# A chunked mLSTM with two feed-forward layers: the state's output matmuls move to the scores, the state update to the outputs, and a second chunk opens with six half-width blocks

## The chip, the core and the metric

The kernel runs on one core of one Trainium2 chip. The metric is the device time of one execution in microseconds (us), the median of the runs shown; less is better. Before the change it is 881.96 us over 3 runs (881.24 to 885.67). TensorE is written PE (its weight loads PEld), VectorE DVE, ScalarE ACT, GpSimd POOL, and SP is the queue that issues the DMAs.

## The reference

```python
for t in range(S):                        # B, H, S, D = 4, 8, 768, 40
    m_new = np.maximum(f_gate[:, :, t] + m, i_gate[:, :, t])
    f_stab = np.exp(f_gate[:, :, t] + m - m_new)
    i_stab = np.exp(i_gate[:, :, t] - m_new)
    C = f_stab * C + i_stab * np.einsum('bhd,bhe->bhde', vt, kt)
    n = f_stab * n + i_stab * kt
    h_tilde = np.einsum('bhde,bhe->bhd', C, qt)
    denom = np.maximum(np.abs(np.einsum('bhd,bhd->bh', n, qt)), 1.0)
    y[:, :, t] = sigmoid(o_gate[:, :, t]) * h_tilde / denom
x = y as (3072 tokens, 320)
x = (sigmoid(x @ w_gate) * (x @ w_val)) @ w_out            # d_ff 1536
h = x @ w_in
out = (h * clip(h + 3, 0, 6) / 6) @ w_out2                 # d_ff 2048
```

## The kernel before

The 768 tokens are cut into 6 chunks (0 to 5) of 128; with 4 batches that is 24 pieces of attention, each over 8 heads. Inside a chunk the recurrence is a masked product; between chunks a state of 40 x 41 words for each head (`cst`; the 41st column is the normaliser) is carried. All attention matmuls take fp32 operands; those of the feed-forward layers take fp32r words split into a high and a low part.

One piece of attention (chunk c, batch b) is three functions. They are called here by letters:

- **S** (`att0`, line 299): the scores, 8 matmuls of 40 x 128 by 128 columns, in two PSUM banks, one for even and one for odd heads (L303). DVE makes the decay matrix `dec` by two scans (L320, after a DMA that spreads a row over the partitions), scales v into `vi` and `vd`, and multiplies the scores into `dec` (L333).
- **I** (`att1`, line 340): for c > 0 the state's output part **O**, 16 matmuls with 32 output rows and 82 columns (L349): two heads' queries are stacked in 128 rows, and `cst` holds the two heads' states side by side with zero blocks. Then the chunk's own output, 32 matmuls of 41 columns (L360). DVE adds both into `y` (L373, L376), divides and gates it into `yo` (L380 to L387).
- **T** (`att2`, line 397): three transposes of `yo` (L402); then the state update **C**, 8 matmuls with 40 output rows (L409). ACT and DVE write the transposed piece as high and low part `xh`, `xl` (L419, L420), and DVE renews `cst` in two halves (L429, L432).

The first feed-forward layer goes over 12 hidden blocks for each chunk. One block of one chunk is a **step**: 16 matmuls for gate and value (`m1_h`, L443 to L450), ACT's sigmoid and DVE's product `g` (L470), a split into `gh` and `gl` (L456, L457), and one step later 8 matmuls into three accumulators (`m1_out`, L485, L495). In chunks 0 and 1 the first 4 blocks are done by halves (256 columns: batches 0 and 1, then batches 2 and 3), so that a chunk can begin before its last two batches are ready. `quota` says how many pieces of attention are emitted ahead of each step; from chunk 2 on it is one a step, and the pieces are a chunk ahead of the feed-forward layer. The order of pieces is (c,b) S, (c,b-1) T, (c,b) I.

During chunk 0 the weights are also converted: 64-bit words come in through SP, and ACT and DVE make fp32 and split it (L105 to L154). The second feed-forward layer (L601 on) begins when all chunks have gone through the first, with no attention beside it.

PSUM's 8 banks are three pools: 3 `mm` for `m1_h`, 3 `acc`, and 2 `att` for attention. The tiles `qk`, `vko` and `dec` of a piece have two buffers each; the loads for a piece are emitted behind T of the piece two before it and go out on SP in the order `qk`, `dec`, `vko`, each when its buffer is free. Each engine runs its instructions in the order in which a scheduler has written them when the kernel is built. These lines set the half-width blocks and the pieces:

```python
halves = 4
n = halves if c < 2 else 0
quota = [2, 2] + [1] * 4 + [0, 1] * 4 + [1] * (n_first - 14)
quota += [1] * (len(steps) - len(quota))
```

Of the kernel before, what the change touches and what calls it, by code (L numbers as in the profile page):

```python
# [8 lines left out]
F32 = mybir.dt.float32  # L9
# [10 lines left out]
L = 128  # L20
NC = S // L
# [11 lines left out]
def mlstm_then_two_gated_ffn(  # L33
# [33 lines left out]
    def any_ps():  # L67
        k = banks_used[0] % 8
        banks_used[0] += 1
        return ps_mm() if k < 3 else ps_acc() if k < 6 else ps_att()  # L70
# [7 lines left out]
    cst = const.tile([P, B, NP, 2 * D1], F32, name="cst")  # L78
# [191 lines left out]
    nc.gpsimd.memset(cst, 0.0)  # L270
# [26 lines left out]
    def att0(c, b, ps):  # L297
        a = at[c, b]
        qk, dec = a["qk"], a["dec"]
        s_ps = [ps(), ps()]  # L300
        for h in range(H):
            p0 = 64 * (h % 2)
            nc.tensor.matmul(  # L303
                out=s_ps[h % 2][:, (h // 2) * L : (h // 2 + 1) * L],
                lhsT=qk[p0 : p0 + D, 1, h // 2, :],
                rhs=qk[p0 : p0 + D, 0, h // 2, :],
                start=h < 2,
                stop=h >= H - 2,
                skip_group_check=True,
            )  # L310
        vko_t = a["vko"]
        vi = ap.tile([P, H, D1], F32, tag="vi", name="vi")
        v_h = vko_t[:, 0, :].rearrange("p (h d) -> p h d", d=D)
# [12 lines left out]
        a["vi"] = vi  # L326
        if c < NC - 1:
            vd = ap.tile([P, H, D1], F32, tag="vd", name="vd")
            scale_heads(vd, vi, dec[:, :, L - 1 : L], c == 0 and b > 0)
            a["vd"] = vd  # L330
        for n in range(2):
            x = dec.rearrange("p (n two) l -> p two n l", two=2)[:, n]
            nc.vector.tensor_tensor(  # L333
                out=x, in0=s_ps[n].rearrange("p (n l) -> p n l", l=L), in1=x, op=ALU.mult
            )

        with tc.issue_after(first_exp):
            nc.scalar.activation(out=vko_t[:, 2, :], in_=vko_t[:, 2, :], func=AF.Sigmoid)

    def att1(c, b, ps):  # L340
        a = at[c, b]
        dec, vi = a["dec"], a["vi"]

        halves = [slice(t, t + 32) for t in range(0, L, 32)]
        if c > 0:
            o_ps = ps()
            for n in range(NP):
                for tt in halves:
                    nc.tensor.matmul(  # L349
                        out=o_ps[tt, n * 2 * D1 : (n + 1) * 2 * D1],  # L350
                        lhsT=a["qk"][:, 0, n, tt],
                        rhs=cst[:, b, n, :],
                        start=n == 0,
                        stop=n == NP - 1,
                        skip_group_check=True,
                    )
        i_ps = ps()
        for h in range(H):
            for tt in halves:
                nc.tensor.matmul(  # L360
                    out=i_ps[tt, h * D1 : (h + 1) * D1],
                    lhsT=dec[:, h, tt],
                    rhs=vi[:, h, :],
                    start=h == 0,
                    stop=h == H - 1,
                    skip_group_check=True,
                )
        i_v = i_ps[:, : H * D1].rearrange("p (h d) -> p h d", d=D1)
        y = ap.tile([P, H, D1], F32, tag="y", name="y")
        den = ap.tile([P, H, 1], F32, tag="den", name="den")  # L370
        if c > 0:
            o_v = o_ps[:, : H * D1].rearrange("p (h d) -> p h d", d=D1)
            nc.vector.tensor_tensor(  # L373
                out=y, in0=o_v, in1=gT[:, c, b].to_broadcast([P, H, D1]), op=ALU.mult
            )
            nc.vector.tensor_tensor(out=y, in0=y, in1=i_v, op=ALU.add)  # L376
        else:
            nc.scalar.copy(out=y, in_=i_v)
# [6 lines left out]
        scale_heads(y[:, :, 0:D], y[:, :, 0:D], den, c == 1 or c == 0 and b < 2)  # L385
# [9 lines left out]
        a["yo"] = yo  # L395

    def att2(c, b, ps):
        a = at.pop((c, b))
        yo = a["yo"]
        x_ps = ps()  # L400
# [4 lines left out]
        if c < NC - 1:  # L405
            c_ps = ps()
            for h in range(H):
                p0 = 64 * (h % 2)
                nc.tensor.matmul(  # L409
                    out=c_ps[p0 : p0 + D, (h // 2) * D1 : (h // 2 + 1) * D1],  # L410
                    lhsT=a["vko"][:, 1, h * D : (h + 1) * D],
                    rhs=a["vd"][:, h, :],
                    start=h < 2,
                    stop=h >= H - 2,
                    skip_group_check=True,
                )
# [6 lines left out]
        if c < NC - 1:  # L423
            for j in range(2):
                pp = slice(64 * j, 64 * j + D)
                cv = cst[pp, b, :, j * D1 : (j + 1) * D1]
                c_v = c_ps[pp, : NP * D1].rearrange("p (n d) -> p n d", d=D1)
                if c > 0:
                    nc.vector.tensor_tensor(  # L429
                        out=cv, in0=cv, in1=gend[pp, c, b].to_broadcast([D, NP, D1]), op=ALU.mult  # L430
                    )
                    nc.vector.tensor_tensor(out=cv, in0=cv, in1=c_v, op=ALU.add)  # L432
                else:
                    nc.scalar.copy(out=cv, in_=c_v)
# [133 lines left out]
    halves = 4  # L568

    def tile_steps(c):  # L570
        n = halves if c < 2 else 0
        by_half = [(c, f, slice(j * T // 2, (j + 1) * T // 2)) for j in range(2) for f in range(n)]
        return by_half + [(c, f, slice(0, T)) for f in range(n, F1)]
# [11 lines left out]
    quota = [2, 2] + [1] * 4 + [0, 1] * 4 + [1] * (n_first - 14)  # L585
    quota += [1] * (len(steps) - len(quota))
    before = []
    for i, (c, f, ts) in enumerate(steps):
        if i == halves - 1:
            for b in range(2):  # L590
                att_load(1, b)
                dec_load(1, b)
        for _ in range(quota[i]):
            if pieces:
# [3 lines left out]
                (att0, att1, att2)[piece](cp, b, ps_att)  # L598
# [10 lines left out]
        if c == 0:  # L609
            work(1 if i < 2 * halves else 2, n_w1)  # L610
# [79 lines left out]
def _layout(q, k, v, i_gate, f_gate, o_gate, moe_w_gate, moe_w_val, moe_w_out, moe2_w_in, moe2_w_out):  # L690
# [21 lines left out]
    def words(w):  # L712
# [6 lines left out]
        "vko": np.stack([tokens(v), tokens(k), tokens(o_gate)], axis=3),  # L719
# [26 lines left out]
```

## Time and profile before

| | |
|---|---|
| median of 3 runs | 881.96 us |
| the profiled execution: its own time, its span | 883.74 us, 881.8 us |
| PE busy, weight loads busy | 844.9 us (96%), 721.9 us (82%) |
| DVE busy | 536.0 us (61%) |
| ACT busy | 362.2 us (41%) |
| mean share of the 16 DMA engines' bandwidth moved | 96 GB/s |

How to read it: the busy time of PE has the pipelined ends of matmuls in it, so that 96% does not mean that PE could do no more; the distance from one matmul's start to the next is what a matmul costs in a row. The span has four stretches: until 41.66 us the first pieces of attention alone; until 132.14 us chunk 0 of the first layer, with the conversion of weights; until 537.81 us its other chunks, which have attention beside them up to 461 us; and then the second layer.

### The profile page before, as it was taken

To read this page: it belongs to the slowest core of one execution; us is meant where nothing else is said; L and a number is where in the kernel's file an instruction comes from. 1 tells how busy PE (TensorE), PEld (TensorE's weight loads), DVE (VectorE), ACT (ScalarE), POOL (GpSimd) and SP (SyncE) were. 2 spreads that over 40 slices of the span, in tenths; PEclk is the share of its full clock that TensorE was granted. 3 is DMA by queue.
4 is the path that set the end of the run, shared out by engine and by line. 5 is a ranking of instruction groups with operands and counts; after the bars stand their busy time and mean duration, and the time that the engine had idled before them with its cause. 6 is when DMAs were issued, how large, how long until landed. Compare 5 with 4: busy or idle time off the path is not lost.

```text
span 881.8 us, 16306 instructions
## 1 busy us (share of the span) xinstructions
PE 844.9 (96%) x6805; PEld 721.9 (82%) x6805; DVE 536.0 (61%) x955; ACT 362.2 (41%) x728; POOL 2.5 (0%) x8
## 2 busy tenths in 40 slices
PE   2699998999999999999999999999999999999998
PEld 2587777887778778788888888999999999999997
DVE  7999997666777786777645554434343353443443
ACT  5874654222332233242325445334343343433433
POOL 1000000000000000000000000000000000000000
PEclk9999999999999999999999999999999999999999
DMA  9745453232443544435302231001010010000000
GB/s 324 269 143 183 149 184 130 83 108 71 150 143 135 183 159 153 161 132 196 135 1 71 90 105 72 1 1 66 1 56 11 1 66 1 30 1 1 30 1 30
DMA packets 25208, 84.43 MB, mean 96 GB/s; under 512 B 2608, under 2 KB 5872, under 8 KB 25136
## 3 DMA queue, kind: packets, MB, share of 16 engines
q1 hardware_dynamic: 25088, 83.31, 27.4%
q8 instruction: 53, 0.87, 0.4%
q14 instruction: 19, 0.16, 0.1%
q10 hardware_dynamic: 48, 0.10, 0.0%
HBM read 69.40 MB, written 13.99 MB: 95 GB/s over the span
## 4 chain that ended last, share of the span: by engine, by line
PE 82%; DVE 11%; DMA 3%; ACT 2%; issue 1%; SPq 0%; DVEq 0%; ACTq 0%
PE mm L447 11%; PE mm L449 11%; PE mm L448 11%; PE acc L485 9%; PE mm L443 6%; PE mm L450 5%; PE acc L652 5%; PE acc L651 5%; PE acc L650 5%; PE acc L495 3%; PE att L303 2%; DVE dec L320 2%; PE att L652 2%; PE att L651 2%; PE att L650 2%
## 5 line engine op out<-in xcount | busy, mean ns | idle before, releaser
L447 PE MATMUL mm<-xh,w 128*128 128x512 f32 (+1 forms) x512 | 194.4, 380 | 0.0
L449 PE MATMUL mm<-xh,w 128*128 128x512 f32 (+1 forms) x512 | 193.9, 379 | 0.0
L448 PE MATMUL mm<-xl,w 128*128 128x512 f32 (+1 forms) x512 | 193.8, 378 | 0.0
L456 ACT CAST gh<-g 128x512 fp32r<-128x512 f32 (+1 forms) x176 | 105.7, 600 | 177.3 <-PE att L651 90.2
L457 DVE TENSOR_TENSOR gl<-g,gh 128x512 fp32r<-128x512 f32 (+1 forms) x176 | 117.2, 666 | 99.9 <-ACT gh L456 99.5
L632 DVE SCALAR_TENSOR_TENSOR g<-g,mm 128x512 f32<-128x512 f32 x96 | 66.0, 688 | 112.0 <-ACT g L631 112.0
L449 PEld LDWEIGHTS mm<-xh,w 128*128 128x128 f32 x512 | 97.1, 190 | 18.9
L631 ACT ACTIVATE g<-mm,half 128x512 f32<-128x512 f32 x96 | 66.2, 690 | 112.1 <-PE mm L450 112.1
L448 PEld LDWEIGHTS mm<-xl,w 128*128 128x128 f32 x512 | 97.0, 190 | 18.5
L447 PEld LDWEIGHTS mm<-xh,w 128*128 128x128 f32 x512 | 97.0, 190 | 14.3
L485 PE MATMUL acc<-gh,w 128*128 128x512 f32 (+1 forms) x320 | 104.5, 371 | 1.6 <-ACT gh L456 1.6
L443 PE MATMUL mm<-xl,w 128*128 128x512 f32 (+1 forms) x256 | 103.5, 404 | 0.1
L450 PE MATMUL mm<-xh,w 128*128 128x512 f32 (+1 forms) x256 | 96.6, 377 | 0.0
L469 ACT ACTIVATE g<-mm 128x512 f32<-128x512 f32 (+1 forms) x80 | 44.3, 554 | 121.3 <-PE mm L450 121.3
L652 PE MATMUL acc<-w,gl 128*128 128x320 f32 x288 | 89.0, 309 | 0.0
L651 PE MATMUL acc<-w,gh 128*128 128x320 f32 x288 | 88.9, 309 | 0.0
L650 PE MATMUL acc<-w,gh 128*128 128x320 f32 x288 | 88.8, 308 | 0.0
L470 DVE TENSOR_TENSOR g<-g,mm 128x512 f32<-128x512 f32 (+1 forms) x80 | 50.3, 629 | 55.5 <-PE mm L450 54.9
L485 PEld LDWEIGHTS acc<-gh,w 128*128 128x128 f32 x320 | 59.9, 191 | 12.1 <-ACT gh L456 2.0
L485 PE MATMUL acc<-gl,w 128*128 128x512 f32 (+1 forms) x160 | 59.7, 374 | 2.7 <-DVE gl L457 2.7
L320 DVE TENSOR_TENSOR_SCAN dec<-dec,ident 128x512 f32<-128x512 f32 x44 | 52.0, 1212 | 9.4 <-DMA dec<-fz_dram 9.4
L443 PEld LDWEIGHTS mm<-xl,w 128*128 128x128 f32 x256 | 48.2, 188 | 9.9 <-DVE xl L420 0.2
(145 smaller groups left out, 1092.1 us busy)
## 6 DMA issues: line engine op xcount, KB each, us to landing
raw<-in_w SPq DMA_DIRECT2D x20, 640.0 KB, 4.6
qk<-in_qkT SPq DMA_DIRECT2D x22, 512.0 KB, 4.7
dec<-fz_dram SPq DMA_DIRECT2D x22, 512.0 KB, 5.8
vko<-in_vko SPq DMA_DIRECT2D x22, 480.0 KB, 4.2
raw<-in_wo SPq DMA_DIRECT2D x14, 640.0 KB, 4.0
w_dram<-bits SPq DMA_DIRECT2D x16, 320.0 KB, 3.6
raw<-w_dram SPq DMA_DIRECT2D x16, 320.0 KB, 3.0
x_dram<-x SPq DMA_DIRECT2D x6, 768.0 KB, 4.9
```

Source lines behind the costliest of these rows:

```text
L320: nc.vector.tensor_tensor_scan(out=x, data0=x, data1=ident4.rearrange("p h l -> p (h l)"), initial=0.0, op0=ALU.mult, op1=ALU.add,)
L443: nc.tensor.matmul(out=banks[j], lhsT=tail, rhs=xl[:, 2, :], start=True, stop=False)
L447: nc.tensor.matmul(out=banks[j], lhsT=hi, rhs=xh[:, k, :], start=False, stop=False)
L448: nc.tensor.matmul(out=banks[j], lhsT=hi, rhs=xl[:, k, :], start=False, stop=False)
L449: nc.tensor.matmul(out=banks[j], lhsT=lo, rhs=xh[:, k, :], start=False, stop=False)
L450: nc.tensor.matmul(out=banks[j], lhsT=tail, rhs=xh[:, 2, :], start=False, stop=True)
L456: nc.scalar.copy(out=gh, in_=g)
L457: nc.vector.tensor_tensor(out=gl, in0=g, in1=gh.bitcast(F32), op=ALU.subtract)
L485: nc.tensor.matmul(out=a[m], lhsT=lhsT, rhs=rhs, start=st and lhsT is hi and rhs is gh, stop=en and lhsT is lo, skip_group_check=True,)
L650: nc.tensor.matmul(out=a, lhsT=gh[:, ts], rhs=hi, start=st, stop=False)
L651: nc.tensor.matmul(out=a, lhsT=gh[:, ts], rhs=lo, start=False, stop=False)
L652: nc.tensor.matmul(out=a, lhsT=gl[:, ts], rhs=hi, start=False, stop=en)
```

## The change

Every part, in the order of the diff (S, I, T, O, C as above):

- PSUM: `mm` gets 4 banks, `att` 1. S takes its banks as `mm, mm, mm, att` (with O) or `mm, att`, I as `att, mm`, T as `mm`.
- O goes to the front of S and becomes 32 matmuls, one for each head and quarter of the tokens, with 40 rows and 41 columns; its results stay apart for even and odd heads, and DVE multiplies them by the decay in two operations. `cst` loses its zero blocks (and POOL its memset).
- The scores become 32 matmuls with 32 output rows each, so that O and scores have one shape of tile, 64 rows by 32 columns (8 tiles in the array).
- C goes from T to the end of I and becomes 16 matmuls with 32 output rows (two for each head, the second with rows that nobody reads; k now stands ahead of v in `vko` so that the last one stays inside). DVE renews `cst` in one operation for all 128 partitions each, in I.
- T is the three transposes and the split alone.
- Chunk 1, the second, begins with 6 blocks by halves in place of 4; `quota` has two steps without a piece there. In chunk 1 the division of `y` of batches 2 and 3 goes from ACT (8 operations) to DVE (1).

```diff
-    mm_ps = ctx.enter_context(tc.tile_pool(name="mm_ps", bufs=3, space=PSUM))
+    mm_ps = ctx.enter_context(tc.tile_pool(name="mm_ps", bufs=4, space=PSUM))
-    att_ps = ctx.enter_context(tc.tile_pool(name="att_ps", bufs=2, space=PSUM))
+    att_ps = ctx.enter_context(tc.tile_pool(name="att_ps", bufs=1, space=PSUM))
-    cst = const.tile([P, B, NP, 2 * D1], F32, name="cst")
+    cst = const.tile([P, B, NP, D1], F32, name="cst")
...
-    def att0(c, b, ps):
+    def att0(c, b, banks):
...
+        quarters = [slice(t, t + 32) for t in range(0, L, 32)]
+        if c > 0:
+            o_ps = [banks(), banks()]
+            for n in range(NP):
+                for tt in quarters:
+                    for j in range(2):
+                        pp = slice(64 * j, 64 * j + D)
+                        nc.tensor.matmul(
+                            out=o_ps[j][tt, n * D1 : (n + 1) * D1],
+                            lhsT=qk[pp, 0, n, tt],
+                            rhs=cst[pp, b, n, :],
...
+            for j in range(2):
+                o_v = o_ps[j][:, : NP * D1].rearrange("p (n d) -> p n d", d=D1)
+                heads = slice(j, H, 2)
+                nc.vector.tensor_tensor(
+                    out=y[:, heads, :], in0=o_v, in1=gT[:, c, b, heads, :].to_broadcast([P, NP, D1]),
+                    op=ALU.mult,
+                )
+        s_ps = [banks(), banks()]
+        for n in range(NP):
+            for ss in quarters:
+                for j in range(2):
+                    pp = slice(64 * j, 64 * j + D)
+                    nc.tensor.matmul(
+                        out=s_ps[j][ss, n * L : (n + 1) * L],
+                        lhsT=qk[pp, 1, n, ss],
+                        rhs=qk[pp, 0, n, :],
...
-    def att1(c, b, ps):
+    def att1(c, b, banks):
...
+        if c < NC - 1:
+            c_ps = banks()
+            for h in range(H):
+                for d in range(0, 64, 32):
+                    p0 = 64 * (h % 2) + d
+                    nc.tensor.matmul(
+                        out=c_ps[p0 : p0 + 32, (h // 2) * D1 : (h // 2 + 1) * D1],
+                        lhsT=k_t[:, h * D + d : h * D + d + 32],
+                        rhs=a["vd"][:, h, :],
...
-        scale_heads(y[:, :, 0:D], y[:, :, 0:D], den, c == 1 or c == 0 and b < 2)
+        scale_heads(y[:, :, 0:D], y[:, :, 0:D], den, c == 1 and b < 2 or c == 0 and b < 2)
...
+            if c > 0:
+                nc.vector.tensor_tensor(
+                    out=cv, in0=cv, in1=gend[:, c, b].to_broadcast([P, NP, D1]), op=ALU.mult
+                )
+                nc.vector.tensor_tensor(out=cv, in0=cv, in1=c_v, op=ALU.add)
...
-    halves = 4
+    halves = (4, 6)
...
-    quota = [2, 2] + [1] * 4 + [0, 1] * 4 + [1] * (n_first - 14)
+    quota = [2, 2] + [1] * 4 + [0, 1] * 4 + [1] * (n_first - 14) + [1, 1, 0, 1, 0, 1]
...
+    def banks_of(c, piece):
+        if piece == 0:
+            return in_turn([ps_mm, ps_mm, ps_mm, ps_att] if c else [ps_mm, ps_att])
+        return in_turn([ps_att, ps_mm] if piece == 1 else [ps_mm])
```

What the scheduler makes of it, at three places. **First, PE in the later chunks, where I stands between two steps.** L485 and L495 (now L496 and L506) are the end of a step, L443 (now L454) the begin of the next; L349 is O, L360 (now L375) the chunk's own output, L389 is C.

```order
L495 MATMUL acc<-gl,w 64x512
L495 MATMUL acc<-gh,w 128x512
L349 MATMUL att<-cst,qk 32x82 x16
L360 MATMUL att<-vi,dec 32x41 x32
L443 MATMUL mm<-xl,w 128x512
```

```order
L506 MATMUL acc<-gl,w 64x512
L506 MATMUL acc<-gh,w 128x512
L375 MATMUL att<-vi,dec 32x41 x32
L389 MATMUL mm<-vd,vko 32x41 x16
L454 MATMUL mm<-xl,w 128x512
```

O has left this place, and C has come to it in twice as many matmuls.

**Second, DVE in chunk 1, behind I of batch 3**: L387 (now L413) makes that batch's `yo`, L320 (now L347) are the two scans of the piece (2,1), which wait for a load of `dec`; L457 (now L468) is `gl` of a step, L420 (now L443) is `xl` of batch 3.

```order
L470 TENSOR_TENSOR g<-g,mm 128x256
L387 TENSOR_TENSOR yo<-y,vko 128x320
L457 TENSOR_TENSOR gl<-g,gh 128x256
L320 SCALAR_TENSOR_TENSOR dec<-dec,ident_78 128x512 x2
L420 TENSOR_TENSOR xl<-att,xh 128x3x128
```

```order
L413 TENSOR_TENSOR yo<-y,vko 128x320
L481 TENSOR_TENSOR g<-g,mm 128x256
L347 SCALAR_TENSOR_TENSOR dec<-dec,ident_78 128x512
L468 TENSOR_TENSOR gl<-g,gh 128x256
L347 SCALAR_TENSOR_TENSOR dec<-dec,ident_78 128x512
L481 TENSOR_TENSOR g<-g,mm 128x256
L293 TENSOR_TENSOR vi<-vko,iT 128x8x40
L293 TENSOR_TENSOR vd<-vi,dec 128x328
L468 TENSOR_TENSOR gl<-g,gh 128x256
L443 TENSOR_TENSOR xl<-mm,xh 128x3x128
```

A `gl` that stood ahead of the scans now stands behind the first of them.

**Third, DVE at the last conversion of chunk 0** (L151 and L154 are its end): before, the steps' products are `g` and `gl` of step 14, the last but one of the chunk, and (1,2)'s `y` follows at once.

```order
L470 TENSOR_TENSOR g<-g,mm 128x512
L151 TENSOR_TENSOR w<-bits,w 128x2x64
L154 TENSOR_TENSOR w<-bits,w 128x2x256
L457 TENSOR_TENSOR gl<-g,gh 128x512
L373 TENSOR_TENSOR y<-att,gT 128x328
```

```order
L481 TENSOR_TENSOR g<-g,mm 128x512
L151 TENSOR_TENSOR w<-bits,w 128x2x64
L154 TENSOR_TENSOR w<-bits,w 128x2x256
L468 TENSOR_TENSOR gl<-g,gh 128x512
L443 TENSOR_TENSOR xl<-mm,xh 128x3x128
L481 TENSOR_TENSOR g<-g,mm 128x512
L468 TENSOR_TENSOR gl<-g,gh 128x512
L401 TENSOR_TENSOR y<-y,att 128x328
```

Now the pair around the conversion's end is that of step 13, and step 14's follows: the conversions stand one step earlier among the steps' products.

## Rows read from the trace of the kernel before

**Rows 1.** Windows: chunk 0, chunk 1's opening, the rest with attention; columns in its first line.

```profile
core 0: us, PE busy (x) PEld busy (x) DVE busy (x) ACT busy (x) POOL busy (x), PEclk, DMA share, GB/s
41.66:132.14 90.48, 86.29 (x885) 72.31 (x885) 85.63 (x175) 57.41 (x162) 0.00 (x0) 0.98 0.49 167
132.14:187.08 54.94, 49.30 (x654) 43.50 (x652) 38.80 (x80) 18.43 (x53) 0.00 (x0) 0.97 0.30 100
187.08:461.25 274.17, 274.17 (x2742) 219.09 (x2739) 193.65 (x359) 84.17 (x163) 0.00 (x0) 1.00 0.40 136
```

**Rows 2.** The chain that ended last: where each step's accumulating matmuls start (us, us, what).

```profile
204.80 1.36 PE acc L485 x6
211.24 1.36 PE acc L485 x6
...
407.21 1.36 PE acc L485 x6
413.02 1.36 PE acc L485 x6
414.85 0.71 PE att L349 x32
...
420.05 1.36 PE acc L485 x6
421.87 1.09 PE att L303 x16
426.86 1.36 PE acc L485 x6
...
470.63 1.36 PE acc L485 x6
476.09 1.36 PE acc L485 x6
```

**Rows 3.** Timeline of PE around one I: start us, us, engine, line, operation.

```profile
454.07 0.78 PE L349 MATMUL att<-cst,qk 128*32 128x82 f32 x32
454.67 0.81 PE L360 MATMUL att<-vi,dec 128*32 128x41 f32 x64
455.41 0.50 PE L443 MATMUL mm<-xl,w 128*128 128x512 f32 x1
```

**Rows 4.** Timeline of PE: starts of two half-width steps, and T that waits.

```profile
143.38 0.38 PE L443 MATMUL mm<-xl,w 128*128 128x256 f32 x1
...
146.35 0.28 PE L443 MATMUL mm<-xl,w 128*128 128x256 f32 x1
...
148.91 0.52 PE L402 MATMUL att<-ident,yo 128*128 128x128 f32 x3 [1.45 <-DVE yo L387]
```

**Rows 5.** Groups of instructions on DVE, shapes apart: busy us, mean ns, idle before.

```profile
L457 DVE TENSOR_TENSOR gl<-g,gh 128x512 fp32r<-128x512 f32 x160 | 110.5, 690 | 96.6 <-ACT gh L456 96.2
L470 DVE TENSOR_TENSOR g<-g,mm 128x512 f32<-128x512 f32 x64 | 43.8, 684 | 53.8 <-PE mm L450 53.2
L429 DVE TENSOR_TENSOR cst<-cst,gend 40x164 f32<-40x164 f32 x32 | 10.2, 320 | 0.3
L373 DVE TENSOR_TENSOR y<-att,gT 128x328 f32<-128x328 f32 x20 | 9.9, 494 | 2.3 <-PE att L349 2.3
```

**Rows 6.** Timeline of SP: when two loads of dec are issued, behind I.

```profile
143.48 0.34 SPq L193 DMA_DIRECT2D dec<-fz_dram  x1
...
160.68 1.12 SPq L193 DMA_DIRECT2D dec<-fz_dram  x1
```

**Rows 7.** Timeline of DVE: the scans that wait for those two loads.

```profile
150.15 2.34 DVE L320 TENSOR_TENSOR_SCAN dec<-dec,ident 128x512 f32<-128x512 f32 x2 [1.04 <-DMA dec<-fz_dram]
...
166.34 2.34 DVE L320 TENSOR_TENSOR_SCAN dec<-dec,ident 128x512 f32<-128x512 f32 x2 [1.73 <-DMA dec<-fz_dram]
```

**Rows 8.** Timeline of ACT: the division of y of batch 3 in chunk 1.

```profile
146.38 1.86 ACT L292 ACTIVATE y<-y,den 128x40 f32<-128x40 f32 x8 [1.30 <-DVE den L384]
```

**Rows 9.** The chain in chunk 1: one C, two tiles of 64 columns at work.

```profile
169.91 0.51 PE att L409 x16
```

More of the change, by code (lines that the diff above doesn't have):

```diff
@@ L269, in mlstm_then_two_gated_ffn @@
     nc.gpsimd.memset(fs_sb[:, :S], 0.0)
-    nc.gpsimd.memset(cst, 0.0)
     nc.vector.memset(half, 0.5)
@@ L294, in scale_heads @@
             nc.vector.tensor_tensor(out=out, in0=in_, in1=by.to_broadcast(list(out.shape)), op=ALU.mult)
-    def att0(c, b, ps):
+    def att0(c, b, banks):
         a = at[c, b]
         qk, dec = a["qk"], a["dec"]
[L300 to L310, printed above, removed]
+        quarters = [slice(t, t + 32) for t in range(0, L, 32)]
[9 more added lines that the diff above has]
+                            rhs=cst[pp, b, n, :],
+                            start=n == 0,
+                            stop=n == NP - 1,
+                            skip_group_check=True,
+                        )
+            y = ap.tile([P, H, D1], F32, tag="y", name="y")
+            a["y"] = y
+            for j in range(2):
[14 more added lines that the diff above has]
+                        rhs=qk[pp, 0, n, :],
+                        start=n == 0,
+                        stop=n == NP - 1,
+                        skip_group_check=True,
+                    )
@@ L338, in att0 @@
             nc.scalar.activation(out=vko_t[:, 2, :], in_=vko_t[:, 2, :], func=AF.Sigmoid)
-    def att1(c, b, ps):
+    def att1(c, b, banks):
         a = at[c, b]
[L342 to L357, printed above, removed]
+        dec, vi, k_t = a["dec"], a["vi"], a["vko"].rearrange("p a n -> p (a n)")
+        i_ps = banks()
         for h in range(H):
-            for tt in halves:
+            for t in range(0, L, 32):
                 nc.tensor.matmul(
-                    out=i_ps[tt, h * D1 : (h + 1) * D1],
-                    lhsT=dec[:, h, tt],
+                    out=i_ps[t : t + 32, h * D1 : (h + 1) * D1],
+                    lhsT=dec[:, h, t : t + 32],
                     rhs=vi[:, h, :],
@@ L395, in att1, with att2 @@
         a["yo"] = yo
[L397 to L400, printed above, removed]
+        if c < NC - 1:
+            cv = cst[:, b]
+            c_v = c_ps[:, : NP * D1].rearrange("p (n d) -> p n d", d=D1)
+            if c > 0:
+                nc.vector.tensor_tensor(
+                    out=cv, in0=cv, in1=gend[:, c, b].to_broadcast([P, NP, D1]), op=ALU.mult
+                )
+                nc.vector.tensor_tensor(out=cv, in0=cv, in1=c_v, op=ALU.add)
+            else:
+                nc.scalar.copy(out=cv, in_=c_v)
+    def att2(c, b, banks):
+        yo = at.pop((c, b))["yo"]
+        x_ps = banks()
         for k in range(3):
@@ L404, in att2 @@
             )
[L405 to L416, printed above, removed]
         x_v = x_ps[:, : 3 * P].rearrange("p (k t) -> p k t", k=3)
@@ L422, in att2 @@
         )
[L423 to L434, printed above, removed]
     def h_pair(w, x, banks, ts=slice(0, T)):
@@ L597, in mlstm_then_two_gated_ffn @@
                     x_tiles((1, cp))
-                (att0, att1, att2)[piece](cp, b, ps_att)
+                (att0, att1, att2)[piece](cp, b, banks_of(cp, piece))
                 nxt = divmod(cp * B + b + 2, B)
@@ L609, in mlstm_then_two_gated_ffn @@
         if c == 0:
-            work(1 if i < 2 * halves else 2, n_w1)
+            work(1 if i < 2 * halves[0] else 2, n_w1)
         elif c < NC - 1:
```

27 lines of the change are left out of this document (17 added, 10 removed).

## The prediction

> **What bounds the kernel now.** I read the windows first [rows 1]: from 187.08 us to the end of attention, 274.17 us, PE is busy without a gap at the full granted clock, and DVE for 194 of them. Chunk 0 is otherwise: DVE is busy for 85.63 of 90.48 us, PE has slack. Chunk 1's opening lies between: in 54.94 us neither engine is full, and the granted clock is 0.97 in the mean. So a matmul saved counts in full in the long stretch, hardly in chunk 0, and the opening hangs on waits.
>
> Then the chain of waits [rows 2]. In the long stretch it runs along PE, so the distance from one step's accumulating matmuls to the next's is the price of the step and of what stands in it: 5.46 us plain (476.09 - 470.63); 7.03 with I and its O (420.05 - 413.02), so I with O is 1.57; 6.81 with S, so S is 1.35; 6.44 with T and C (211.24 - 204.80), so 0.98; 5.81 with T alone (413.02 - 407.21), so 0.35. Check: the stretch holds 41 steps, 13 S, 14 I, 10 T with C and 4 without (chunk 5 has none): 223.9 + 17.6 + 22.0 + 9.8 + 1.4 = 274.7, against 274.17 measured. The prices carry.
>
> All sums are changes against the profiled execution (883.74 us, 1.78 above the median) and are put on the median, 881.96. A measurement of this kernel can tell about 0.5%, 4.4 us.
>
> **The change, part by part: the long stretch.**
> - O leaves I: from O's start to the next matmul's start 0.60 us [rows 3]. Fourteen times: -8.4.
> - C leaves T: 0.98 - 0.35 = 0.63, with the change of the array's shape in and out, since the transposes need none [rows 2]. Ten times: -6.3.
> - C comes to I, in I's own shape: half as many matmuls of 41 columns as the chunk's own output, which takes 0.74 to the next step's start [rows 3]. So at most 0.37; I take 0.35. Ten times: +3.5.
> - O comes to S. No row shows 8 tiles at once. Below: the same columns on twice as many tiles as now, half of 0.60, 0.30. Above: as many matmuls of the same width as the chunk's own output on 4 tiles, 0.74 [rows 3]. I take the middle, 0.50. Thirteen times: +6.5, from 3.9 to 9.6.
> - The scores in 32 matmuls for 8: the same columns on the same part of the array, and 32 matmuls at that pace need 0.74, less than the 1.09 they take now [rows 2, 3]. So 0; a smaller first weight load could give back 0.1 each, 1.3 in all.
> - On DVE O's product becomes two of 164 columns (about 0.32 each for 0.49) and `cst` two operations of 0.32 for four [rows 5]. DVE has 80 us to spare here, so nothing. POOL's memset and ACT's second copy of `cst` in chunk 0 lie beside other work too. Were that cover gone, a piece would save 0.5 us.
> - Banks: a step takes the banks of the scores and of O that stood before the previous step. DVE empties them within some 3 us, a step lasts 5.46, so nothing with full steps.
>
> Sum: -8.4 - 6.3 + 3.5 + 6.5 = **-4.7 us**, with O's bounds from -7.3 to -1.6.
>
> **Chunk 0 and the opening.** A half-width step is 146.35 - 143.38 = 2.97 us [rows 4]; two halves cost 0.48 more than a full step. Before, the opening (132.14 to 187.08, when T of piece (2,1) is done) holds 8 halves, 2 full steps, 4 T with C, 3 I, 3 S: 23.8 + 10.9 + 3.9 + 4.7 + 4.1 = 47.4, and 7.6 of stalls [rows 1]. One is shown: T of batch 3 waits for `yo` [rows 4], behind 1.86 us of divisions on ACT [rows 8]. Now the same work is 12 halves, 4 T, 3 I with C (1.57 - 0.60 + 0.35 = 1.32) and 3 S with O (1.85): 35.6 + 1.4 + 4.0 + 5.6 = 46.6. So the work itself gives -0.8.
>
> What stalls next is DVE's order (second place shown with the change). The load of `dec` goes out when I has ended and is there 6.7 and 5.7 us later [rows 6, 7]. A scan that waits for it holds up all of DVE behind it, and the `gl` of the step just done now stands behind the first scan: ready 5.7 to 6.7, plus 1.2, plus 0.4 after I, that is 7.3 to 8.3. PE asks for it after C, two gate parts (1.98 each) and one output part (0.99): 5.3. So a stall of 2.0 to 3.0 behind I of (1,3); behind I of (2,0) and (2,1) an S of 1.85 lies between, so 0.1 to 1.1 each. There the next step also takes the scores' bank, which DVE frees only behind both scans and five more operations: about 1.4 each. Together 2.5 + 1.0 + 2.8 = 6.3 for 7.6 before: -1.3. The division on DVE, 0.49 for 1.86, takes the shown stall away, and `vko` comes sooner, since I frees it and no longer T; both are in this sum.
>
> The third place costs something. DVE is full in chunk 0, so its order decides. Now the last conversion stands beside step 13's `g` and no longer 14's. From that `gl` PE still has the rest of an output part (1.6), I with C (1.3), a gate part (3.65), an output part (1.8) and S with O (1.85) before the first half-width block, 10.2 us; before it was an output part and S, 3.0. So +7.2. DVE reaches the place sooner: one `g` and `gl` less (1.4), `cst` three operations less (1.0), against six products of O for two (0.9) [rows 5]; `xl` against `vd` cancel: -1.4. And of the 4.85 us in which DVE idled in chunk 0 [rows 1] I let 2 go, because the products that waited stand later. Net +3.8. Then the first half-width block needs the bank that `g` of step 15 frees, which stands behind two waiting scans: 5.7 + 2.3 + 0.7 = 8.7 after I, where PE is there after 7.7: +0.9.
>
> Together -0.8 - 1.3 + 3.8 + 0.9 = **+2.6 us** (from -5 to +10, see the rivals). Total -4.7 + 2.6 = -2.1: **880 us**.
>
> **The rivals.**
> 1. *The forecast, 880* (876 to 884): the gain of the long stretch half given back at chunk 0's end. Chance 0.42.
> 2. *The opening is relieved, 872.* DVE does not reach the last conversion late, since all its work but order is lighter: the hand-over costs nothing, and the stalls halve, 3.8 for 7.6. -4.7 - 0.8 - 3.8 = -9.3, and 0.8 more from the weight loads. For it: DVE idles 16 of 55 us in the opening [rows 1], and the slack steps in `quota` lie where T waited. Against it: the order, in which loads now hold up `gl`. Chance 0.30.
> 3. *DVE's wait for `dec` eats everything, 888.* Every load takes 6.7, DVE saves only its 1.4 in chunk 0 (hand-over 5.8 + 1.9), stalls 9.5 for 7.6, and the clock falls once more: a mean of 0.97 over 55 us, between the two levels of 1.2 and 2.4 GHz, is 3.3 us at the lower, 1.6 lost. -0.8 + 5.8 + 1.9 + 1.9 + 1.6 = +10.4, with -4.7: +5.7. It decides from the point at which the opening ends 4.7 us later than now, at 191.8. For it: DVE in order, full in chunk 0. Against: each load but one has an S between. Chance 0.24.
> 4. *Small matmuls pay a floor each, 915.* If the 64 matmul records of O (two for each fp32 matmul) and of the scores were paced as C is now, 0.51 us for 16 [rows 9], each would be 2.0 us: 1.5 more for O and 0.7 for the scores, 16 times, +35. Against it: the chunk's own output does 64 records in 0.74, 12 ns each [rows 3]. Chance 0.04. The Trainium skill ("TensorEngine Tiling (Array Packing)", Instruction Overhead) gives each matmul an overhead of about 60 cycles; by that, as an estimate at 2.4 GHz, 25 ns, O would take 1.6 and the scores 1.6, some +25 us in all and about 905. The 12 ns of rows 3 disagree with it for 4 tiles; no run here shows 8.
>
> That the change might not do what it says is no case: the order shows O, C and the steps where they were put.
>
> **How the numbers follow.** The range reaches into 2 and 3 and leaves out rival 4, the upper end of 3 and the lower of 2: 868 to 889. Faster by over 0.5% is below 877.6: all of rival 2 and a quarter of the forecast (the short end of O), 0.41. Within 0.5%: the rest of the forecast and a third of rival 3, 0.39. Slower, over 886.4: the rest, 0.20.
>
> **What would show it.** Steps in the long stretch of 7.3 with S, 6.8 with I and C, 5.8 with T; O in S about 0.5. The first half-width block of chunk 1 at about 137 us where it is 132.14 now. `gl` behind a scan, with PE waiting some 2 us behind I of (1,3). T in the opening without a wait for `yo`. The forecast is wrong if O's 8 tiles cost over 0.74, or if the first full step behind (2,1)'s T starts before 184 or after 194 (189.7 is forecast).

## The result and the profile after

The changed kernel takes 889.15 us (median of 8 runs, 887.54 to 892.13) where the kernel before took 882.45 (8 runs) beside it: a ratio of 1.0072, with a 95% interval of 1.0053 to 1.0091. The forecast was 880, its range 868 to 889; the time went the other way, and the interval leaves no doubt of the direction. The profiled execution took 888.52 us, its span is 886.7.

Three stretches, from the windows of the changed kernel; they answer to [rows 1], and each begins and ends at the same work as there.

```profile
core 0: us, PE busy (x) PEld busy (x) DVE busy (x) ACT busy (x) POOL busy (x), PEclk, DMA share, GB/s
46.48:144.16 97.68, 91.37 (x1416) 76.74 (x1412) 87.87 (x179) 56.85 (x155) 0.00 (x0) 0.95 0.44 150
144.16:193.17 49.01, 46.65 (x977) 43.98 (x973) 35.08 (x81) 14.79 (x39) 0.00 (x0) 1.00 0.37 124
193.17:466.13 272.96, 270.46 (x3910) 215.15 (x3908) 184.59 (x349) 83.17 (x163) 0.00 (x0) 1.00 0.40 133
```

So the ledger against the kernel before, in us of the spans (the last column is the best kernel of the experiments, and the one ahead of it mends the change's two new waits):

| stretch | forecast | the change | both edits | best |
|---|---|---|---|---|
| until the first half-width block (before 41.66) | 0 | +4.8 | +1.6 | +1.6 |
| chunk 0 (90.48) | +4.7 | +7.2 | +6.8 | +3.0 |
| opening of chunk 1 (54.94) | -2.1 | -5.9 | -7.2 | -6.8 |
| long stretch (274.17) | -4.7 | -1.2 | -5.2 | -5.2 |
| the rest (420.55) | 0 | 0.0 | +0.1 | 0.0 |
| sum | -2.1 | +4.9 | -4.0 | -7.4 |

Two lines stand out. The first was not in the forecast at all: the start is 4.8 us later. And the long stretch, in which PE was busy without a gap before, gives back most of its gain.

**The long stretch: the prices came as forecast.** From the chain of waits of the changed kernel (start, us, what), where each step's accumulating matmuls start:

```profile
197.10 0.71 PE acc L496 x6
198.04 0.75 PE att L375 x64
...
202.93 1.36 PE acc L496 x6
204.75 0.68 PE mm L308 x58
...
210.28 1.36 PE acc L496 x6
212.10 0.33 PE mm L437 x3
216.10 1.36 PE acc L496 x6
217.93 0.75 PE att L375 x64
...
222.83 1.36 PE acc L496 x6
```

A step with S and O is 210.28 - 202.93 = 7.35 (forecast 7.3), with T 216.10 - 210.28 = 5.82 (5.8), with I and C 222.83 - 216.10 = 6.73 (6.8). These answer to [rows 2].

**But some steps are longer.** From the list of waits of the changed kernel (what waited for what: us in total, times, longest): DVE's scans (L347) wait 27.7 us for `dec`, and PE waits ahead of a step's matmuls for gate or value (L454) for O's product on DVE (L321) and for the step product `g` (L481).

```profile
DVE dec L347 <- DMA dec<-fz_dram: 27.7, 16, 3.5
...
PE mm L454 <- DVE y L321: 3.0, 6, 1.0
...
PE mm L454 <- DVE g L481: 1.7, 3, 0.9
```

In the long stretch by itself the same list gives 1.7 us for `g` (three times) and 0.8 us for O's product (three times); another 1.6 us for O's product lies in the opening. In the kernel before the scans waited 9.4 us, a third of 27.7 (a line of its page):

```profile
L320 DVE TENSOR_TENSOR_SCAN dec<-dec,ident 128x512 f32<-128x512 f32 x44 | 52.0, 1212 | 9.4 <-DMA dec<-fz_dram 9.4
```

One such place, on DVE's timeline of the changed kernel (start, us, line, operation, and in brackets what it waited for):

```profile
244.90 1.23 DVE L347 TENSOR_TENSOR_SCAN dec<-dec,ident 128x512 f32<-128x512 f32 x1 [2.81 <-DMA dec<-fz_dram]
246.04 0.66 DVE L481 TENSOR_TENSOR g<-g,mm 128x512 f32<-128x512 f32 x1
246.62 1.22 DVE L347 TENSOR_TENSOR_SCAN dec<-dec,ident 128x512 f32<-128x512 f32 x1
247.75 0.67 DVE L468 TENSOR_TENSOR gl<-g,gh 128x512 fp32r<-128x512 f32 x1
248.34 0.56 DVE L321 TENSOR_TENSOR y<-mm,gT 128x164 f32<-128x164 f32 x2
```

The chain runs through that load there (start, us, what):

```profile
238.55 0.14 PE mm L389 x16
238.68 6.19 DMA dec<-fz_dram
...
244.90 0.04 DVE dec L347
244.94 1.10 issue
246.04 0.67 DVE g L481
```

The load goes out as I ends (whether I or SP's queue held it until then is asked in experiment 4) and takes 6.19 us, and on DVE the scan that waits for it has `g`, `gl` and O's two products behind it. The step right behind S needs two banks that these free: S takes three of the four `mm` banks, so the step takes the value bank of the step just done, which `g` frees, and then O's even bank. Here PE waits for `g`, and the step from 238.78 to 246.76 takes 7.98 us for 7.31; elsewhere it waits for O's product. Over the long stretch such steps hold some 4 us.

**The start.** Piece (0,1)'s scores and its I, PE's timeline of the changed kernel, against the same matmuls before (L303 there, I is L360; (0,1)'s I writes `mm`):

```profile
10.73 1.95 PE L330 MATMUL att<-qk 40*32 40x128 f32 x30
...
27.43 0.69 PE L437 MATMUL acc<-ident,yo 128*128 128x128 f32 x2 [3.08 <-DVE yo L413]
28.05 1.49 PE L330 MATMUL acc<-qk 40*32 40x128 f32 x18
...
33.17 1.32 PE L375 MATMUL mm<-vi,dec 128*32 128x41 f32 x64 [2.11 <-DVE dec L360]
```

```profile
11.45 1.92 PE L303 MATMUL att<-qk 40*128 40x128 f32 x14
...
22.28 0.37 PE L360 MATMUL mm<-vi,dec 128*32 128x41 f32 x8
...
23.73 1.19 PE L360 MATMUL mm<-vi,dec 128*32 128x41 f32 x56
```

Before, both score banks of (0,1) are `att` banks, and I follows, 8 records at 22.28 and the rest at 23.73. Now there is one `att` bank; the even scores take an `acc` bank, whose turn comes after C and T of (0,0), and T waits for `yo` until 27.43. All of I of (0,1) comes at 33.17, 9.4 us behind the bulk of it before.

### The profile page after: what moved, and what is told of

Read it like the earlier page. It is cut to its first block, busy times and chain, and to the rows that moved or that the text cites. A ratio compares the mean times of both kernels' runs of the same rounds, so it can differ in the third digit from the quotient of the medians.

```text
span 886.7 us, 20534 instructions
## 1 busy us (share of the span) xinstructions
PE 845.4 (95%) x8965; PEld 722.7 (82%) x8965; DVE 527.3 (59%) x949; ACT 357.7 (40%) x712; POOL 1.4 (0%) x7
## 4 chain that ended last, share of the span: by engine, by line
PE 83%; DVE 8%; DMA 6%; issue 2%; ACT 1%; DVEq 0%; SPq 0%; ACTq 0%
PE mm L458 11%; PE mm L460 11%; PE mm L459 11%; PE acc L496 10%; PE mm L454 6%; PE mm L461 6%; DMA dec<-fz_dram 5%; PE acc L677 5%; PE acc L676 5%; PE acc L675 5%; PE acc L506 3%; DVE dec L347 2%; PE att L375 2%; PE att L677 2%; PE att L676 2%
## 5 line engine op out<-in xcount | busy, mean ns | idle before, releaser
L459 PE MATMUL mm<-xl,w 128*128 128x512 f32 (+1 forms) x520 | 195.1, 375 | 0.0
L468 DVE TENSOR_TENSOR gl<-g,gh 128x512 fp32r<-128x512 f32 (+1 forms) x178 | 117.4, 660 | 101.3 <-ACT gh L467 100.9
L459 PEld LDWEIGHTS mm<-xl,w 128*128 128x128 f32 x520 | 98.9, 190 | 18.3
L460 PEld LDWEIGHTS mm<-xh,w 128*128 128x128 f32 x520 | 98.8, 190 | 18.4
L458 PEld LDWEIGHTS mm<-xh,w 128*128 128x128 f32 x520 | 99.0, 190 | 13.7
L454 PE MATMUL mm<-xl,w 128*128 128x512 f32 (+1 forms) x260 | 105.3, 405 | 4.7 <-DVE y L321 3.0
L496 PE MATMUL acc<-gh,w 128*128 128x512 f32 (+1 forms) x328 | 105.1, 366 | 1.7 <-ACT gh L467 1.6
L481 DVE TENSOR_TENSOR g<-g,mm 128x512 f32<-128x512 f32 (+1 forms) x82 | 50.5, 616 | 65.4 <-PE mm L461 64.4
L496 PEld LDWEIGHTS acc<-gh,w 128*128 128x128 f32 x328 | 60.8, 190 | 11.8 <-ACT gh L467 2.0
L347 DVE TENSOR_TENSOR_SCAN dec<-dec,ident 128x512 f32<-128x512 f32 x44 | 53.0, 1217 | 27.8 <-DMA dec<-fz_dram 27.7
L496 PE MATMUL acc<-gl,w 128*128 128x512 f32 (+1 forms) x164 | 60.6, 370 | 4.4 <-DVE gl L468 4.4
L454 PEld LDWEIGHTS mm<-xl,w 128*128 128x128 f32 x260 | 49.3, 190 | 18.2 <-DVE y L321 6.0
```

Of the source, the lines that this page charges most:

```text
L347: nc.vector.tensor_tensor_scan(out=x, data0=x, data1=ident4.rearrange("p h l -> p (h l)"), initial=0.0, op0=ALU.mult, op1=ALU.add,)
L454: nc.tensor.matmul(out=banks[j], lhsT=tail, rhs=xl[:, 2, :], start=True, stop=False)
L458: nc.tensor.matmul(out=banks[j], lhsT=hi, rhs=xh[:, k, :], start=False, stop=False)
L459: nc.tensor.matmul(out=banks[j], lhsT=hi, rhs=xl[:, k, :], start=False, stop=False)
L460: nc.tensor.matmul(out=banks[j], lhsT=lo, rhs=xh[:, k, :], start=False, stop=False)
L468: nc.vector.tensor_tensor(out=gl, in0=g, in1=gh.bitcast(F32), op=ALU.subtract)
```

## The experiments

The kernel before ran beside each; its medians lay between 882.7 and 883.2, so ratios are given where a small difference decides.

**1. The order of banks at the start** (changed kernel, one line):

```diff
-        return ps_mm() if k < 4 else ps_acc() if k < 7 else ps_att()
+        return ps_acc() if k in (3, 4, 5) else ps_att() if k == 6 else ps_mm()
```

> Of the changed kernel only the order in which the first pieces of attention take PSUM's banks is altered, so that the two score banks of (0,1) no longer stand in the queue of the acc banks behind T of (0,0). Theory: the late start (first half-width block at 46.5 us, before 41.7) comes from that queue alone; I of (0,1) starts near 24 us in place of 33.2, the first half-width block at 41.5 to 43, and because DVE is full in chunk 0 the gain is kept: the first half-width block of chunk 1 near 140 in place of 144.2, time 884 to 886. Rival: the start is late because C now stands ahead of T and its state copy ahead of y on ACT; then the first block stays at 46 and the time at 889. Second rival: the start is earlier but chunk 0's order of conversions and products takes it back; first block 42, chunk 1 at 144, time 889.

Measured: 883.74 us (10 runs), ratio to before 1.0006 [0.9985, 1.0026]. The bulk of I of (0,1) starts at 23.8, the first half-width block at 42.68, that of chunk 1 at 139.06: 5.1 of 5.4 us gained are there at chunk 1. The theory holds, and a term of nearly 5 us that stood in no sum is found.

**2. The same queue put into the kernel before:**

```diff
-        return ps_mm() if k < 3 else ps_acc() if k < 6 else ps_att()
+        return ps_mm() if k < 3 else ps_acc() if k in (3, 4, 6) else ps_att()
```

> The kernel BEFORE the change, with one edit: the order of banks at the start is altered so that the even score bank of (0,1) stands in the acc pool behind T of (0,0), as the change has it. Theory: this queue by itself makes the late start and nothing else of the change is needed: the first half-width block comes at 45 to 47 in place of 41.7, DVE is full in chunk 0 so that the delay is carried to the end, time 886 to 888. Rival: the kernel before has the slack of DVE's 4.85 idle us in chunk 0 to take it up: time 883 to 885, though the first block is late.

Measured: 886.03 us (10 runs), 1.0032 [1.0015, 1.0048]. PE's timeline of this kernel has the picture of the changed one, T, then scores, then I:

```profile
29.65 0.97 PE L402 MATMUL acc<-ident,yo 128*128 128x128 f32 x3 [6.09 <-DVE yo L387]
30.55 2.07 PE L303 MATMUL acc<-qk 40*128 40x128 f32 x8
...
34.33 1.32 PE L360 MATMUL mm<-vi,dec 128*32 128x41 f32 x64 [1.03 <-DVE dec L333]
```

The first block comes at 46.49, that of chunk 1 at 136.40 (+4.3), the whole time is 3.3 us longer. So the queue alone, without anything else of the change, makes the late start; most of it reaches the end, somewhat less than from the changed kernel.

**3. Scans behind O's products, from piece (2,2) on** (changed kernel):

```diff
+                last_o = nc.vector.tensor_tensor(
...
-        for n in range(2):
+        with tc.issue_after(last_o) if c * B + b >= 10 else nullcontext():
+            for n in range(2):
...
```

> Of the changed kernel only this is altered: from piece (2,2) on, the two scans stand on DVE behind the two products of O of the same piece, where some of those stand behind a scan now. Theory: the 4.3 us of extra time in full steps of the long stretch (steps of 7.98, 8.34, 6.46, 6.39 for 7.31 and 5.84) is PE waiting for O's bank behind a scan that waits for the load of dec; so every S step becomes 7.3, every T step 5.84, the stretch from (2,1)'s T to 466 us falls from 273.0 to about 269, time 885. Rival: the wait only moves: the scans end later, I then waits for dec, the steps with I grow to 7.5 or more, and the time stays at 889.

Measured: 884.17 us (10 runs), 1.0009 [0.9992, 1.0025]. The group of scans now waits 3.2 us for `dec` in all, and the long stretch is full again:

```profile
193.19:462.18 268.99, 268.99 (x3906) 215.65 (x3907) 188.66 (x352) 83.84 (x163) 0.00 (x0) 1.00 0.41 135
```

4.0 us less than 272.96, as expected. The place shown above reads so now (DVE):

```profile
245.29 0.56 DVE L321 TENSOR_TENSOR y<-mm,gT 128x164 f32<-128x164 f32 x2 [0.38 <-PE mm L308]
245.77 2.33 DVE L347 TENSOR_TENSOR_SCAN dec<-dec,ident 128x512 f32<-128x512 f32 x2
```

The scans start 0.9 us later than the first of them did, and wait for nothing; O's products are 3.0 us sooner, and `g`, which the edit also takes from behind the scan, 3.2 (242.84 for 246.04). So the run shows the cost of readers behind a waiting scan, not which of the two readers cost how much; for that there are only the waits above. The rival (I waits in turn) is refuted: steps with I stay at 6.72.

**4. A third buffer for `dec`** (changed kernel):

```diff
-            d = ap.tile([P, H, L], F32, tag="dec", name="dec")
+            d = ap.tile([P, H, L], F32, tag="dec", name="dec", bufs=3)
```

> Of the changed kernel only the number of buffers of dec is altered, from two to three. Theory: a load of dec goes out only when I of the piece two before has read the buffer; with a third it goes out with the piece's other loads, the scans' wait for dec falls from 27.7 us in all to under 10, the steps of 8 us in the long stretch vanish, and the time is 884 to 886. Rival: the load is held on SP by the order of its queue (it stands behind vko's or qk's, or behind T of two pieces before), the waits stay over 20 and the time at 889.

Measured: 888.88 us (4 runs), 1.0077 [1.0052, 1.0103]; the scans wait 28.0 us. The rival's time holds, though what stands ahead in the queue is none of the things that it named. SP's timeline at the same place:

```profile
238.23 0.33 SPq L88 DMA_DIRECT2D raw<-in_wo  x1
239.52 0.33 SPq L531 DMA_DIRECT2D w_dram<-bits  x1
239.93 0.39 SPq L193 DMA_DIRECT2D dec<-fz_dram  x1
```

The load goes out 0.4 us behind a store of converted weights, and that store right behind the end of DVE's last conversion operation (L116, 238.67 to 239.49): with its buffer free the load is as late as without. In the changed kernel the same load stands 0.42 us behind the same store (238.26 and 238.68), just as I ends, so there both the buffer and the queue could have held it. Here the third buffer did not help, since the queue had not got to the load.

**5. Both edits, 1 and 3.**

> The two edits of the runs before together (order of banks at the start, and from (2,2) on the scans behind the products of O). Theory: they lie in different stretches, the first shifts all by 5.1 to 5.4, the second shortens the long stretch by 4: 878.5 to 880. Rival: what the first gains is partly the same wait for dec, so the sum falls short: 882 to 884.

Measured: 879.02 us (4 runs), 0.9959 [0.9945, 0.9974]. They add: the sum of the two gains, 5.4 + 5.0, would give 878.8. That this is near the forecast of 880 is in part luck: by the ledger its start and chunk 0 are 3.7 us dearer than forecast, its opening 5.1 cheaper.

**6. Chunk 0: the conversions put back behind the products.** Two forms. In the first each conversion of chunk 0 gets an edge (an order that the scheduler must keep) behind its step's `g`; in the second, on the full-width steps only, there is one conversion a step, behind that step's `gl`.

```diff
+        product = nc.vector.tensor_tensor(out=g, in0=g, in1=banks[1], op=ALU.mult).ins
...
-            work(1 if i < 2 * halves[0] else 2, n_w1)
+            with tc.issue_after(product):
+                work(1 if i < 2 * halves[0] else 2, n_w1)
```

```diff
+        split_g.last = nc.vector.tensor_tensor(out=gl, in0=g, in1=gh.bitcast(F32), op=ALU.subtract).ins
...
-            work(1 if i < 2 * halves[0] else 2, n_w1)
+            with tc.issue_after(split_g.last) if i >= 8 else nullcontext():
+                work(1, n_w1)
```

> Of the changed kernel only this is altered: in chunk 0 each step's conversion of weights stands on DVE behind that step's product g, as the order had it before the change by itself. Theory: the conversions ahead of the products are what makes the hand-over long; from the last conversion's end to the first half-width block of chunk 1 is 13.4 us now and becomes 5 to 7; the block comes near 138 to 140 in place of 144.2, time 883 to 885. Rival: DVE is full in chunk 0, so that the last conversion only ends later by what the products gain; the block stays within 1 us of 144.2 and the time at 889. Nothing changes behind 193 us by either but the shift.

> Of the changed kernel only the conversions at the end of chunk 0 are altered: from the first full-width step on, one conversion a step in place of two, each on DVE behind gl of its own step, so that one conversion more than now stands behind the gl of step 11 (for which PE waits at 119.7 us). Theory: what PE still has to do behind that gl until chunk 1 is fixed, some 24 us, so whatever stands ahead of it on DVE delays chunk 1; with one conversion (about 3.6 us of DVE) less ahead of it the first half-width block comes at 139 to 141.5 in place of 144.2 and the time is 884 to 886.5. Rival: DVE is full, the last conversions then end later, and step 15 waits for its own weights; the block stays within 1.5 of 144.2, time 888 to 889.5.

Measured: 892.30 us (6 runs), 1.0098 [1.0068, 1.0128], and 888.72 us (8 runs), 1.0073 [1.0051, 1.0096]. Both misses. With the first, from the start of the last conversion's last operation (L154) to chunk 1 is 9.2 us in place of 13.4 (the expectation says its end; 13.4 is from its start), but the conversion itself is 10 us later: already the first of chunk 0's fifteen, which now waits for a product, is split (L137) 11 us later, at 55.83 for 44.86. With the second that distance is 4.0, and chunk 1 still begins at 144.10: PE's timeline shows that step 15 then waits for its own weights.

```profile
139.65 0.50 PE L496 MATMUL acc<-gh,w 128*128 128x512 f32 x1 [1.61 <-ACT w L150]
140.86 0.73 PE L496 MATMUL acc<-gh,w 128*128 128x512 f32 x2 [0.48 <-DVE w L154]
```

**7. Scans behind O's products in all pieces** (edit 1, and edit 3 with `c > 0`), without and with the second form of 6:

> As the run with both, but the scans stand behind the products of O in every piece of chunks 1 to 5, so also in chunk 0's end and in the opening. Theory: what lengthens chunk 0's end is the gl of step 11, which stands behind a conversion and a scan on DVE (PE waits 3.0 us for it and then runs at the lower clock; step 12 takes 12.3 for about 8); with the scans out of its way the step takes 8 to 10, the first half-width block of chunk 1 comes at 135 to 137 in place of 139.1, and the time is 875 to 877. Rival: DVE is full in chunk 0, so the order of scans is worth nothing there, the block stays at 139 and the time at that of both. Second rival: I now waits for scans that come a step later, the opening grows, and the time is 880 or more.

> The same edit of the conversions on top of the run with the banks' order and all scans behind the products of O. Theory: its first half-width block, 137.9 now, comes at 133 to 135.5, and the time is 874 to 876.5. Rival: its DVE is as full, the block stays at 137 to 139, time 878 to 879.5.

Measured: 878.57 us (10 runs), 0.9968 [0.9950, 0.9986], and 883.09 us (10 runs), 1.0009 [0.9986, 1.0032]. The first has its first block of chunk 1 at 137.90, 2.6 earlier than with both edits, yet its `gl` of step 11 still comes late, behind conversions (PE waits 1.36 us for it), and the opening is 1.1 us longer, with an I that waits 0.93 us for `dec`, a small part of what the second rival said; the time is that of both. The second is 4.5 us slower and a miss: its first block comes at 139.53, and step 15 waits 1.75 us for its own weights, so as in 6 the conversions come too late.

**8. Half way: one conversion a step, no edge** (on top of both edits):

```diff
-            work(1 if i < 2 * halves[0] else 2, n_w1)
+            work(1, n_w1)
```

> The run with both edits, and in addition one conversion a step to the end of chunk 0 in place of two, without any further edge: the fifth conversion then stands behind the gl of step 11 and the last one just ahead of step 14's g, half way between the order of the change and the one tried with all conversions behind gl. Theory: chunk 0's end lies between two limits, gl behind conversions and weights that come late, and half way neither bites: PE's wait for step 11's gl falls from 4.0 to under 2.5, step 15 waits for no weights, the first half-width block of chunk 1 comes at 136 to 139 in place of 140.5, time 875 to 878. Rival: what chunk 0 lasts doesn't hang on this order at all, 139.5 to 141.5, time 878.5 to 880.

Measured: 876.25 us (6 runs), 0.9932 [0.9917, 0.9947], faster than either kernel. PE's waits for step 11's `gh` and `gl` with both edits, and its wait for `gl` now:

```profile
111.82 0.73 PE L496 MATMUL acc<-gh,w 128*128 128x512 f32 x2 [1.34 <-ACT gh L467]
...
115.38 0.79 PE L496 MATMUL acc<-gl,w 128*128 128x512 f32 x1 [2.62 <-DVE gl L468]
```

```profile
111.57 0.50 PE L496 MATMUL acc<-gl,w 128*128 128x512 f32 x1 [0.64 <-DVE gl L468]
```

Chunk 1 begins at 136.67 for 140.49. So the place of the conversions does count, and of the orders tried this is the best, with late `gl` on one side and late weights on the other. The edit moves the conversion on ACT too, where the wait for `gh` is gone; how much of the 3.8 us belongs to ACT's order and how much to DVE's isn't shown. Nor was the same edit tried in the kernel before, so 876.25 says what this kernel can reach and not what the change by itself is worth.

**9. The opening, one part undone at a time** (changed kernel): the half-width blocks back to four with the old `quota`, and the division of batches 2 and 3 in chunk 1 back on ACT.

```diff
-    halves = (4, 6)
+    halves = (4, 4)
...
-    quota = [2, 2] + [1] * 4 + [0, 1] * 4 + [1] * (n_first - 14) + [1, 1, 0, 1, 0, 1]
+    quota = [2, 2] + [1] * 4 + [0, 1] * 4 + [1] * (n_first - 14)
```

```diff
-        scale_heads(y[:, :, 0:D], y[:, :, 0:D], den, c == 1 and b < 2 or c == 0 and b < 2)
+        scale_heads(y[:, :, 0:D], y[:, :, 0:D], den, c == 1 or c == 0 and b < 2)
```

> The changed kernel with 4 half-width blocks at the head of chunk 1 and the quota of before, all else as changed. Theory: chunk 0 is the same to its end (first half-width block of chunk 1 near 144.2), and the opening, 49.0 us now to the first full step behind T of (2,1), loses part of its gain: 51 to 53, time 891 to 893. Rival: what emptied the opening of stalls is not the count of half-width blocks but the lighter pieces (division on DVE, C with I); then the two blocks fewer give back their 0.5 us each and the time is 888. Second rival: the opening grows by over 5 us and the whole time passes 894.

> Of the changed kernel only the division of y of batches 2 and 3 in chunk 1 is put back on ACT (8 operations of 41 columns in place of one on DVE). Theory: it is what lets T in the opening start without a wait; with it back, T of (1,3) waits some 1.4 us again, the opening is 50.5 to 51 us in place of 49.0 and the time 890 to 891. Rival: C with I and the loads that come sooner relieved the opening, not the division: 889 and an opening within 0.5 of 49.0.

Measured: 889.27 us (4 runs), 1.0056 [1.0035, 1.0076], and 887.91 us (4 runs), 1.0063 [1.0048, 1.0078]. Neither part by itself relieved the opening: with the division on ACT it is 48.5 us, and T waits for nothing; with four half-width blocks all of chunk 1 takes 87.7 us (143.28 to 230.99), with six 87.9 (144.16 to 232.05). Each undone alone, the six blocks and the moved division are worth nothing that can be measured here; undoing both was not tried.

## Why the prediction failed, step by step

Against the forecast the span is 7.0 us longer (+4.9 for -2.1): +4.8 at the start, +2.5 in chunk 0, +3.5 in the long stretch, and -3.8 in the opening.

- **Prices of the long stretch: right.** -5.2 us without waits (experiment 3), forecast -4.7. From step starts where nothing waits, O in S is 7.31 - 5.46 - 1.35 = 0.50, as taken (0.54 read directly, in the last section), and C in I is 6.72 - 6.41 = 0.31 for 0.35 (6.41 is a step with I and no C).
- **"Banks: nothing with full steps": this step failed.** It had a step take banks of an S that "stood before the previous step", and let DVE empty them within 3 us, from its operations' durations alone. The step right behind S takes the bank that the last `g` frees and O's even bank of that very S. And a bank is free when DVE's order comes to its reader, and a scan that waits for `dec` stood ahead of `g` and of O's products. I had made this very argument for `gl` in the opening and did not carry it to these two. Price: 4.0 us by experiment 3, 1.7 us of it seen as PE's wait for `g` and 0.8 for O's product.
- **The start: left out.** I listed the pools and the banks taken in turn, but costed them only in steady state. The change of pool sizes also altered which pool the first pieces draw from. Price: 5.4 us by experiment 1 and 3.3 by experiment 2, in the kernel before. The order showed it: the scores of (0,1) stood behind T of (0,0). With both edits the start is still 1.6 us later than before; the granted clock of that stretch is 0.82 there and 1.00 before, but no run tried whether that is the reason.
- **Chunk 0 (+4.7, measured +7.2): the distance near, the mechanism right only in part.** The last conversion's end is 3.0 us later, not 3.4 earlier; without the late start it is 2.1 earlier. From it to chunk 1 it is 9.1 us more, forecast 8.1. Experiment 8 shows that moving one conversion behind `gl` wins 3.8 of that; experiment 6 that moving more shortens the distance and wins nothing, since the conversions then come later. That the way was long only because of the order is therefore too simple. The best kernel's chunk 0 is still 3 us longer than before, and why stays open.
- **The opening (-2.1): better than forecast, for a reason I missed.** It is 49.0 us with 2.4 of stalls where I summed 6.3. I took 6.7 and 5.7 us for the load of `dec` from [rows 6, 7]. They were loads beside another: before, `qk` went out 0.6 us ahead of `dec`; now S is the last reader of `qk`, so that goes out long before. SP in the changed kernel, and the scans that waited:

```profile
144.29 0.33 SPq L189 DMA_DIRECT2D qk<-in_qkT  x1
...
155.05 0.33 SPq L193 DMA_DIRECT2D dec<-fz_dram  x1
...
170.94 0.33 SPq L193 DMA_DIRECT2D dec<-fz_dram  x1
```

```profile
159.57 1.23 DVE L347 TENSOR_TENSOR_SCAN dec<-dec,ident 128x512 f32<-128x512 f32 x1 [1.61 <-DMA dec<-fz_dram]
160.72 0.40 DVE L468 TENSOR_TENSOR gl<-g,gh 128x256 fp32r<-128x256 f32 x1
...
174.68 1.22 DVE L347 TENSOR_TENSOR_SCAN dec<-dec,ident 128x512 f32<-128x512 f32 x1 [0.85 <-DMA dec<-fz_dram]
```

  155.05 to 159.57 is 4.5 us, 170.94 to 174.68 is 3.7. `gl` does stand behind the scan, as forecast, but PE waits 0.75 us for it behind I of (1,3), not 2. The rest of the 2.4 is two waits for O's product behind S of (2,1) and (2,2), 0.57 and 1.03, where I had 1.0 for `gl` and 2.8 for the scores' bank. T waits for nothing, as forecast, though not because of the division (experiment 9). That the separate `qk` load is what makes `dec`'s faster is read from the two traces; no run tried it.
- **Rival 3** had the right time, 888, by the wrong way: it let the opening grow. The opening shrank; the loss lay in the start and in the wait for `dec` in full steps, which it did not name.
- **Rival 4** is refuted. The page of the Trainium skill that I cited with it ("TensorEngine Tiling (Array Packing)", Instruction Overhead) would by my estimate give 1.6 us for O; it takes 0.54, in the last section.

The two signs that the prediction named for being wrong did not come: O stayed under 0.74, and the first full step behind (2,1)'s T starts at 193.17, within 184 to 194. Neither watched the start or the full steps. With the two failed steps mended the kernel takes 879.0 us: the long stretch then has the gain that was forecast, and the rest of the agreement with 880 is in part luck (experiment 5).

## What to carry to other kernels

When a change takes banks or buffers from other pools, follow each pool's turn from the first instruction on and not only in the steady state: a tile drawn from another pool stands in that pool's queue. A bank or buffer is free when the reader's place in its engine's order comes, so look for what can wait ahead of it there, a load above all. And move the waiting instruction behind the one that frees something, before adding a buffer.

## What the runs showed of the hardware

- **O's records go faster on eight tiles than the chunk's own output on four.** PE's timeline of the changed kernel at one S:

```profile
230.40 0.75 PE L308 MATMUL mm<-cst,qk 40*32 40x41 f32 x62
230.94 0.29 PE L330 MATMUL mm<-qk 40*32 40x128 f32 x1
```

  From O's first record to the first of the scores it is 230.94 - 230.40 = 0.54 us, for 64 records 8.4 ns each, where the chunk's own output, as many records of as many columns on 4 tiles, takes 12 [rows 3]. The scores' 64 records take 1.11 us from there to the next step at 232.05, for 1.09 in 16 records before [rows 2]: as forecast nothing, and their smaller weight loads give nothing back. O's tiles have fewer rows too, 40 for 128, so that the number of tiles alone makes the difference isn't shown.
- **A wait cost twice in chunk 0.** Behind PE's 2.14 us wait for `gl` the matmuls of 512 columns follow each other at 0.42 us, where 0.23 is the distance elsewhere:

```profile
119.73 0.60 PE L496 MATMUL acc<-gl,w 128*128 128x512 f32 x1 [2.14 <-DVE gl L468]
120.13 0.63 PE L496 MATMUL acc<-gh,w 128*128 128x512 f32 x1
120.56 0.63 PE L496 MATMUL acc<-gl,w 128*128 128x512 f32 x1
```

  The granted clock is 1.00 from 113.14 to 119.70, with PE busy and then waiting, 0.61 to 121.00 and 0.50 to 122.50, so it fell to the lower level, 1.2 GHz, behind the wait. Not every wait did this: behind the 0.75 us in the opening the clock stays at 1.00. Chunk 0's mean is 0.95 in the changed kernel, 0.94 with both edits and 0.97 in the best one.
